# A fused attention and feed-forward kernel: the first two batches' w_in product by seven multiplications, part of it made ahead and kept in DRAM, and the opening loads re-dealt

## The chip, the cores and the metric

The kernel runs on one core of one Trainium2 chip. The metric is the device time of one execution in microseconds (us). Engines are TensorE (PE in the profile; PEld is its weight loading), VectorE (DVE), ScalarE (ACT), GpSimd (POOL) and SyncE (SP), which only issues transfers here.

## The reference, cut to what matters

```python
# q, k, v: (8 batches, 12 heads, 448, 64); w_in (768, 2048) and w_out (2048, 768) come as 64-bit floats
q_n, k_n = rmsnorm(q, g_q), rmsnorm(k, g_k)
attn = softmax(q_n @ k_n.T / 8) @ v
x = attn_out.transpose(0, 2, 1, 3).reshape(8 * 448, 768)
h = x @ w_in
out = (h * sigmoid(h)) @ w_out
```

The kernel walks over 48 *pairs* of heads (six per batch, n = 0 to 47). In each pair TensorE makes scores, weighted sums and transposes, ScalarE the exponentials, VectorE the sums of exponentials and GpSimd the power of the norms. Between them TensorE gets *filler*: x @ w_in of the two batches finished before. Two batches together need 16 x 12 multiplications of a 128 x 128 piece of w_in with x; "seven products" is the scheme that makes a 2 x 2 block product from seven multiplications rather than eight, at the price of additions, some of them of w_in itself (`sum_w_in`), some of x (`sum_x`).

## The kernel before: the parts concerned

w_in comes as 64-bit words and is rounded to 32 bits on the chip in 24 pieces. One rounding is two ScalarE copies ("opening"), three VectorE instructions and one GpSimd addition.

```python
    def round(self):                                             # class Rounder (cut)
        ...
            nc.vector.tensor_scalar(out=dst, in0=dst, scalar1=HIGH_MIN, scalar2=HIGH_MAX, op0=ALU.max, op1=ALU.min)      # L106
            nc.vector.tensor_scalar(out=wi, in0=wi, scalar1=3, scalar2=0x3FFFFFF8, ...)                                 # L109
            nc.vector.scalar_tensor_tensor(out=wi, in0=high, scalar=-(1 << 30), in1=wi, ...)                            # L113
            nc.gpsimd.tensor_tensor(out=wi, in0=wi, in1=low, op=ALU.add)                                                # L117
        while self.load():       # issues the next raw pieces on SyncE's queue (L68)
            pass
```

Row sums of the exponentials, their reciprocal and the division:

```python
    def sums(members, width):
        ...                                          # TensorE: ones x sums of exponentials (L444)
        nc.vector.reciprocal(out=r[0], in_=t)        # L448

    def divide(n, t):
        engine = nc.gpsimd if n < z.NPAIR else nc.vector      # GpSimd in batch 0
        x = xT(*pairs[n])
        engine.tensor_tensor(out=x, in0=x, in1=t, op=ALU.mult)
```

One block by seven products, of which `two` and `five` are the parts; each product goes through one of two banks named mm, and a bank is free again only after the addition or copy that reads it:

```python
        def two(self):
            nc.scalar.copy(self.p1, (yield from self.product("1")))
            plus((yield from self.product("2")), self.p1, self.done[1, 1])     # plus: VectorE

        def five(self, late=0):
            ...
            plus((yield from self.product("6", steps)), p1, u2)
            nc.scalar.copy(p5, (yield from self.product("5", steps)))
            plus((yield from self.product("7", steps)), u2, u3)
            nc.gpsimd.tensor_tensor(out=u2, in0=u2, in1=p5, op=ALU.add)
            nc.gpsimd.tensor_tensor(out=done[2, 2], in0=u3, in1=p5, op=ALU.add)
            plus((yield from self.product("3", steps)), u2, done[1, 2])
            plus((yield from self.product("4", steps)), u3, done[2, 1])
```

For batches 0 and 1, half the blocks were made whole (six matmuls each), beside batches 1 and 2; the other half by seven products:

```python
    def first_two():
        yield from whole(1, early)          # blocks 0-7 of batch 1; those of batch 0 ran beside batch 1
        for c in range(HW):
            sum_x([0, 1], c)
        yield from halves_in([0, 1], late)

    def weights_in(n, point):               # what of w_in is prepared in pair n, at four points of it
        if n < NPAIR:
            count = point == 3
        else:
            count = n < 5 * NPAIR // 2 and point % 2
        for _ in range(count):
            room.w_in.round()
            room.w_in.open()
        ...                                 # sums of w_in in batches 2 and 3
```

Of the kernel before, what the change touches and what calls it, by code (L numbers as in the profile page):

```python
# [13 lines left out]
ALU = mybir.AluOpType  # L14
# [107 lines left out]
class Room:  # L122
# [6 lines left out]
    def __init__(self, nc, pool, w_in, z):  # L129
# [11 lines left out]
        for i in range(self.NC):  # L141
            for c in range(z.NW):
# [3 lines left out]
                low = 6 + number % 2 if late else 16 + number % 2  # L146
# [4 lines left out]
                        (before.get(raw), bits[:, ds(raw * n, n)]),  # L151
                        bits[:, ts(low, self.COLS)],
                    )
                )
                before[raw] = number
# [14 lines left out]
def kernel(  # L170
# [58 lines left out]
    for t, g in ((gq2, g_q), (gk2, g_k)):  # L229
        for half in range(2):  # L230
            nc.scalar.dma_start(t[ds(half * D, D), :], g.rearrange("(d one) -> d one", one=1))
    load(state, 1)
    for i, g in enumerate((g_q, g_k)):
        nc.sync.dma_start(g1[:, i, :], g.rearrange("(one d) -> one d", one=1))
    room = Room(nc, const, w_in, z)
    while room.w_in.load():
        pass
    ident = const.tile([P, P], F32, name="ident")
# [3 lines left out]
    minus_half = const.tile([P, 1], F32, name="minus_half")  # L242
    nc.gpsimd.memset(minus_half, -0.5)
# [14 lines left out]
    nc.vector.scalar_tensor_tensor(  # L258
        out=gains, in0=gq2, scalar=float(D) ** -0.5, in1=gk2, op0=ALU.mult, op1=ALU.mult
# [10 lines left out]
    def arm():  # L270

        own = [dict(st) for st in state]
        r = copy.copy(room)
        r.w_in = copy.copy(room.w_in)
        return dict(
            tc=tc, nc=nc, z=z, pairs=pairs, state=own, load=lambda *a: load(own, *a), room=r,
            ring=ring, w_out=w_out, normal=(normal, rms), ident=ident, ones=ones, minus_half=minus_half, gains=gains,
            out=out,
        )
# [45 lines left out]
def bounded(  # L325
# [110 lines left out]
    def is_single(n):  # L436
        b, hp = pairs[n]
        return hp >= z.NPAIR - 2 and (b == 0 or b % 2 == 1)
# [11 lines left out]
    def divide(n, t):  # L450
        engine = nc.gpsimd if n < z.NPAIR else nc.vector
        x = xT(*pairs[n])
        engine.tensor_tensor(out=x, in0=x, in1=t, op=ALU.mult)
# [108 lines left out]
    def whole(b, blocks):  # L562

        for f in blocks:
            h = bank(S)
            assert room.w_in.rounded >= (f // room.CHUNK + 1) * z.NW
            for c in range(z.NW):
                nc.tensor.matmul(  # L568
                    h, room.w1(c, f), xT(b, c), start=(c == 0), stop=(c == z.NW - 1)
                )  # L570
                yield S
            t = staged()[:, 0:S]
            nc.scalar.activation(t, h, AF.Silu)
            save(f, b * S, t)
# [25 lines left out]
    def part_in(group, m, rows):  # L600

        chunk = 2 * m // room.CHUNK
        assert all((chunk, step) in summed for step in range(4))
# [19 lines left out]
    def halves_in(group, blocks, beside=lambda m: iter(()), begun=()):  # L623

        owed = []
        for m in blocks:
            if m < len(begun):
                rows, part = begun[m]

                late = int(alone and m == 0)  # L630
                columns, skip = part.five(late), 5 * (HW - late) * late
            else:
                rows = [staged() for _ in range(2)]
                part = part_in(group, m, rows)
                columns, skip = chain(part.two(), part.five()), 0
# [3 lines left out]
            for n in columns:  # L639
                count += 1  # L640
                if count > 0 and (count - 1) % each == 0:
                    if count > each:
                        activate(owed)
                    next(aside, None)
# [3 lines left out]
            owed = [(2 * m + i, group[0], rows[i]) for i in range(2)]  # L648
# [116 lines left out]

    def start(group):


        begun = []
        for m in range(2):  # L770
            rows = [staged() for _ in range(2)]
            begun.append((rows, part_in(group, m, rows)))
        return begun


    early, late = range(z.NF // 2), range(HF // 2, HF)

    def first_two():
        yield from whole(1, early)
# [313 lines left out]
```

## Time and profile before

Median 1469.49 us of three executions (1467.93 to 1470.61). The profiled execution has a span of 1465.1 us. From the trace I cut the run at the first score matmul of each pair and counted TensorE's instructions at the costs that the prediction derives (0.376 us for one 448-column product instruction, two of them per f32 matmul); "idle" is the length of a stretch less that work.

| stretch (us) | length | TensorE work | idle |
|---|---|---|---|
| start to first scores | 15.4 | | |
| batch 0 (n = 0 to 5) | 58.4 | 43.0 | 15.5 |
| batch 1 (n = 6 to 11) | 90.7 | 78.3 | 12.4 |
| batch 2 (n = 12 to 17) | 101.2 | 95.6 | 5.6 |
| batch 3 (n = 18 to 23) | 103.7 | 97.1 | 6.5 |
| pair 0 / pair 4 / pair 6 | 9.5 / 12.9 / 18.7 | 5.3 / 8.3 / 10.5 | 4.3 / 4.6 / 8.2 |

A stretch with much idle time has a hole that something other than TensorE makes. The lines of the profile behind this are in the prediction. The list of instructions in time order gives start, length, engine, line, operation, tiles, count. In the list of instructions in time order (start, length, engine, line, operation, tiles, count), the kernel before has its second group of eight score matmuls at

```profile
20.54 1.76 PE L400 MATMUL sc<-work 64*112 64x448 f32 x8
```

1.76 us is the length at full clock; the first eight, at 15.37, took 3.33 us at half clock.

### The profile page before, as it was taken

The page shows a single profiled execution, that of the slowest core. Times are in us where ns is not written, and L with a number is a line of the kernel's source. Part 1 is how long each engine was busy: PE and PEld are TensorE (multiplying, and loading weights), DVE is VectorE, ACT ScalarE, POOL GpSimd, SP SyncE. Part 2 cuts the span into 40 slices and gives each one's busy share as a digit, 9 for nine tenths or more (in the row PEclk, how much of TensorE's full clock was granted, in tenths as well). Part 3 has the DMA queues.
Part 4 walks back from the last instruction along what each step waited for, and adds up shares of the span by engine and source line. Part 5 has one row for each costly group of instructions (what it writes and reads, how often), then busy time and mean ns, then how long its engine had stood idle before and what let it go on. Part 6 is the DMA issues. An engine that isn't in the chain of part 4 may idle for free.

```text
span 1465.1 us, 14059 instructions
## 1 busy us (share of the span) xinstructions
PE 1432.2 (98%) x5048; PEld 698.8 (48%) x5048; DVE 693.9 (47%) x915; ACT 568.7 (39%) x931; POOL 395.5 (27%) x250
## 2 busy tenths in 40 slices
PE   5989999999999999999999999999999999999998
PEld 2334444444444444444444445555555555555554
DVE  4777866656644545744544687722222222222220
ACT  6779886455555455455445344300000000000000
POOL 5765451333233333332332044410000000000000
PEclk9999999999999999999999999999999999999999
DMA  7524432222232223222221157422222222222220
GB/s 220 131 83 136 140 103 75 78 73 66 71 96 73 67 72 98 63 72 87 76 60 67 63 169 240 138 94 79 79 79 79 81 81 84 81 81 86 85 65 25
DMA packets 124660, 135.49 MB, mean 92 GB/s; under 512 B 50660, under 2 KB 106788, under 8 KB 124580
## 3 DMA queue, kind: packets, MB, share of 16 engines
q1 hardware_dynamic: 124260, 134.49, 30.2%
q8 instruction: 42, 0.69, 0.2%
q14 instruction: 38, 0.31, 0.1%
q10 hardware_dynamic: 320, 0.00, 0.0%
HBM read 87.56 MB, written 40.37 MB: 87 GB/s over the span
## 4 chain that ended last, share of the span: by engine, by line
PE 91%; DVE 4%; issue 1%; POOL 1%; ACT 1%; DMA 0%; ACTq 0%; DVEq 0%; POOLq 0%
PE mm L527 36%; PE sc L527 14%; PE sc L400 9%; PE av L416 9%; PE av L527 7%; PE tr L527 7%; PE mm L568 4%; PE tr L386 2%; PE tr L444 1%; PE tr L381 1%; DVE work L428 1%; DVE work L448 1%; DVE rms L298 1%; POOL rms L304 0%; DVE sums_x L475 0%
## 5 line engine op out<-in xcount | busy, mean ns | idle before, releaser
L405 ACT ACTIVATE work<-sc,rms 112x448 f32<-112x448 f32 x384 | 212.3, 636 | 177.7 <-PE sc L400 154.7
L304 POOL TENSOR_TENSOR rms<-rms,minus_half 112x16 f32<-112x16 f32 (+1 forms) x49 | 175.9, 3590 | 292.3 <-DVE rms L300 271.4
L527 PE MATMUL mm<-x,W 128*128 128x448 f32 x552 | 220.8, 541 | 0.7 <-ACT stage L534 0.6
L400 PE MATMUL sc<-work 64*112 64x448 f32 x768 | 173.2, 570 | 1.4 <-ACT work L390 0.7
L527 PE MATMUL mm<-sums_x,W 128*128 128x448 f32 x408 | 165.9, 542 | 0.7 <-DVE stage L478 0.5
L416 PE MATMUL av<-work,rows 112*64 112x448 f32 x768 | 165.7, 552 | 0.0
L428 DVE TENSOR_TENSOR work<-work 112x896 f32<-112x896 f32 x144 | 158.8, 1104 | 1.8
L527 PEld LDWEIGHTS mm<-x,W 128*128 128x128 f32 x552 | 101.8, 190 | 93.1 <-issue 88.0
L547 POOL TENSOR_TENSOR parts<-parts,stage 128x448 f32<-128x448 f32 (+1 forms) x33 | 37.2, 1128 | 314.2 <-DVE parts L478 302.7
L400 PEld LDWEIGHTS sc<-work 64*112 64x112 f32 x768 | 61.8, 175 | 104.5 <-issue 79.4
L527 PEld LDWEIGHTS mm<-sums_x,W 128*128 128x128 f32 x408 | 74.8, 190 | 68.9 <-issue 61.5
L448 DVE RECIPROCAL work<-tr 128x448 f32<-128x448 f32 x25 | 73.9, 2956 | 49.6 <-PE tr L444 49.6
L416 PEld LDWEIGHTS av<-work,rows 112*64 112x64 f32 x768 | 46.6, 136 | 105.9 <-issue 99.5
L547 POOL TENSOR_TENSOR parts<-parts,W 128x384 f32<-128x384 f32 x9 | 9.0, 995 | 307.8 <-DVE parts L478 307.8
L568 PE MATMUL mm<-x,W 128*128 128x448 f32 x192 | 75.9, 541 | 0.0
L534 ACT COPY stage<-mm 128x448 f32<-128x448 f32 (+1 forms) x30 | 15.7, 524 | 150.0 <-PE mm L527 144.0
L478 DVE TENSOR_TENSOR stage<-mm,parts 128x448 f32<-128x448 f32 (+1 forms) x51 | 31.4, 615 | 78.5 <-PE mm L527 51.6
L527 PE MATMUL mm<-W,work 128*128 128x384 f32 x204 | 68.6, 486 | 0.0
L392 DVE TENSOR_SCALAR work<-tr,gains 128x448 f32<-128x448 f32 x36 | 24.6, 684 | 89.3 <-PE tr L386 89.3
L653 ACT ACTIVATE stage<-stage 128x896 f32<-128x896 f32 x56 | 51.2, 945 | 36.8 <-DVE stage L478 35.9
L527 PE MATMUL sc<-W,work 128*128 128x384 f32 x192 | 64.5, 486 | 0.0
L298 DVE TENSOR_REDUCE rms<-qn 112x8 f32<-112x512 f32 x49 | 33.3, 681 | 55.7 <-ACT qn L297 53.5
(159 smaller groups left out, 1898.8 us busy)
## 6 DMA issues: line engine op xcount, KB each, us to landing
hidden<-stage SPq DMA_DIRECT2D x56, 448.0 KB, 2.8
work<-hidden SPq DMA_DIRECT2D x7, 2048.0 KB, 9.0
x<-hidden SPq DMA_DIRECT2D x7, 2048.0 KB, 8.9
W<-in_moe_w_in_dram SPq DMA_DIRECT2D x24, 512.0 KB, 4.1
rows<-in_moe_w_out_dram SPq DMA_DIRECT2D x32, 384.0 KB, 3.4
rows<-in_q_dram SPq DMA_DIRECT2D x48, 224.0 KB, 3.1
rows<-in_k_dram SPq DMA_DIRECT2D x48, 224.0 KB, 3.6
rows<-in_v_dram SPq DMA_DIRECT2D x48, 224.0 KB, 2.7
```

The source lines that it names most:

```text
L298: nc.vector.tensor_reduce(out=rms[:, i], in_=t, axis=AX.X, op=ALU.add)
L304: nc.gpsimd.tensor_tensor(out=flat, in0=flat, in1=half, op=ALU.pow)
L400: nc.tensor.matmul(banks[:, h, 0:S], kT[rows, ts(j, R)], qT[n % 2][rows, :], start=True, stop=True,)
L405: nc.scalar.activation(e[j][:, h, :], banks[:, h, 0:S], AF.Exp, scale=rms[n % 4][:, 1, h, j : j + 1])
L416: nc.tensor.matmul(st["av"][ds(h * D, D), :], st["v"][:, h, j, :], e[j][:, h, :], start=(j == 0), stop=(j == J - 1),)
L428: nc.vector.tensor_tensor(out=t, in0=e[0] if j == 1 else t, in1=e[j], op=ALU.add)
L448: nc.vector.reciprocal(out=r[0], in_=t)
L478: nc.vector.tensor_tensor(out=out, in0=a, in1=b, op=ALU.add)
L527: nc.tensor.matmul(t, self.left(name, s), self.right(name, s), start=s == ends[0], stop=s == ends[1])
L547: nc.gpsimd.tensor_tensor(out=u2, in0=u2, in1=p5, op=ALU.add)
L568: nc.tensor.matmul(h, room.w1(c, f), xT(b, c), start=(c == 0), stop=(c == z.NW - 1))
L653: nc.scalar.activation(t, t, AF.Silu)
```

## The change

Its intent: make the first two batches wholly by seven products (fewer matmuls), of which only products 1 and 2 of two double blocks are made early, beside batch 1, and parked in a DRAM buffer; prepare w_in in other places to match (the last twelve roundings in pairs 13 to 16 in threes, sums of w_in in pairs 12, 13, 17 and 18); divide on VectorE in batch 0 too; drop batch 0's single row sums; and re-deal the small loads of the opening. The diff, cut to its core:

```diff
-    for t, g in ((gq2, g_q), (gk2, g_k)):
-        for half in range(2):
-            nc.scalar.dma_start(t[ds(half * D, D), :], ...)
+    for i, g in enumerate((g_q, g_k)):
+        nc.scalar.dma_start(g1[:, i, :], ...)                # for the branch
     load(state, 1)
-    for i, g in enumerate((g_q, g_k)):
-        nc.sync.dma_start(g1[:, i, :], ...)
...
+    for t, g in ((gq2, g_q), (gk2, g_k)):
+        for half in range(2):
+            nc.gpsimd.dma_start(t[ds(half * D, D), :], ...)  # the gains, now from GpSimd
...
-    nc.vector.scalar_tensor_tensor(out=gains, in0=gq2, scalar=float(D) ** -0.5, in1=gk2, ...)
+    nc.gpsimd.tensor_tensor(out=gains, in0=gq2, in1=gk2, op=ALU.mult)
+    nc.gpsimd.tensor_scalar(out=gains, in0=gains, scalar1=float(D) ** -0.5, ...)
...
     def is_single(n):
-        return hp >= z.NPAIR - 2 and (b == 0 or b % 2 == 1)
+        return hp >= z.NPAIR - 2 and b % 2 == 1
...
     def divide(n, t):
-        engine = nc.gpsimd if n < z.NPAIR else nc.vector
-        engine.tensor_tensor(out=x, in0=x, in1=t, op=ALU.mult)
+        nc.vector.tensor_tensor(out=x, in0=x, in1=t, op=ALU.mult)
...
-    def whole(b, blocks):                                    # removed
+    ahead = dram.tile([AHEAD, P, 2 * S], F32, name="ahead")
+    def make_ahead(group):
+        for m in range(AHEAD):
+            row = staged()
+            yield from part_in(group, m, [row, row]).two()
+            nc.sync.dma_start(ahead[m], row)
...
     def weights_in(n, point):
-        if n < NPAIR:
+        if n < 2 * NPAIR:
             count = point == 3
         else:
-            count = n < 5 * NPAIR // 2 and point % 2
+            count = 2 * NPAIR < n < 2 * NPAIR + 5 and point > 0
...
+        i = n - 2 * NPAIR
+        if i == 0 and point > 1:
+            for step in range(2):
+                sum_w_in(1, 2 * (point - 2) + step)
+        if i in (1, 5, 6):
+            sum_w_in({1: 0, 5: 2, 6: 3}[i], point)
```

Lines of the changed kernel are numbered four or five higher: the products L527 are L531, the additions that empty the banks L482, the division L457, the row sums L449.

## The prediction

> **What bounds the kernel now.** I read the page first, then stretches of time by batch, then the list of instructions in time order at the two ends of batch 0 and at the start of batch 4. On the page:
>
> ```profile
> PE 1432.2 (98%) x5048; PEld 698.8 (48%) x5048; DVE 693.9 (47%) x915; ACT 568.7 (39%) x931; POOL 395.5 (27%) x250
> PEclk9999999999999999999999999999999999999999
> L568 PE MATMUL mm<-x,W 128*128 128x448 f32 x192 | 75.9, 541 | 0.0
> L527 PE MATMUL mm<-x,W 128*128 128x448 f32 x552 | 220.8, 541 | 0.7 <-ACT stage L534 0.6
> ```
>
> TensorE is the bound, but its busy time is padded: these are spans of pipelined matmuls, so 98% is not full speed. What a matmul costs must come from a dense run:
>
> ```profile
> 373.20 4.69 PE L527 MATMUL mm<-x,W 128*128 128x448 f32 x12
> ```
>
> Twelve instructions in 4.69 us, of which the last shows its full 0.54: (4.69 - 0.54)/11 = 0.377 us each. L568 has 192 rows for what the source makes 96 matmuls (16 blocks x 6 steps), so an f32 matmul is two instructions: 0.752 us per matmul. I count TensorE work with this. Scores and weighted sums run two heads side by side (8 instructions in about 1.5 us plus the tail), so a pair of heads needs 32 x 0.188 + 8 transposes x 0.096 = 6.8 us, and 1.5 more in every second pair for the row sums.
>
> Then by batch, the borders being the first score matmul of batches 0 to 5:
>
> ```profile
> core 0: us, PE busy (x) PEld busy (x) DVE busy (x) ACT busy (x) POOL busy (x), PEclk, DMA share, GB/s
> 15.40:73.80 58.40, 53.27 (x252) 19.24 (x253) 40.11 (x53) 47.18 (x90) 44.49 (x23) 0.97 0.53 149
> 73.80:164.50 90.70, 85.57 (x354) 34.75 (x352) 69.61 (x87) 76.19 (x123) 48.74 (x27) 0.96 0.38 113
> 164.50:265.80 101.30, 100.85 (x399) 42.95 (x398) 68.09 (x93) 75.67 (x115) 38.42 (x19) 1.00 0.33 96
> 265.80:369.40 103.60, 102.23 (x405) 42.87 (x404) 66.07 (x77) 55.94 (x90) 38.54 (x20) 1.00 0.25 73
> ```
>
> Counting the instructions of each stretch at the costs above gives TensorE work of 43.0, 78.3, 95.6 and 97.1 us: idle time inside the stretches is 15.5, 12.4, 5.6 and 6.5 us. From batch 2 on each pair loses only about 1 us, so there a matmul added or removed shows in full. Batches 0 and 1 have real holes. The biggest is in the first pair of batch 1 (18.7 us for 10.5 of work), the next in pair 4 of batch 0 (12.95 for 8.3):
>
> ```profile
> 71.65 2.23 POOL L453 TENSOR_TENSOR x<-x,work 128x448 f32<-128x448 f32 x2
> 72.82 2.96 DVE L448 RECIPROCAL work<-mm 128x448 f32<-128x448 f32 x1 [3.87 <-POOL x L453]
> 75.92 2.12 POOL L453 TENSOR_TENSOR x<-x,work 128x448 f32<-128x448 f32 x1 [2.04 <-ACT work L297]
> 77.09 1.24 DVE L109 TENSOR_SCALAR W<-W 128x512 int32<-128x512 int32 x1
> 82.63 1.76 PE L444 MATMUL mm<-work,ones 112*64 112x448 f32 x4 [4.88 <-DVE work L428]
> ```
>
> GpSimd divides x by the row sums only after its slow power (3.7 us) and the q scaling; VectorE's next reciprocal waits for that (it overwrites the divisor), then all of VectorE is late, and TensorE's row sums wait 4.9 us. The clock is granted at 0.82 in this pair. The opening:
>
> ```profile
> 6.59 0.16 DVE L258 SCALAR_TENSOR_TENSOR gains<-gq,gk 128x1 f32<-128x1 f32 x1 [6.59 <-DMA gk<-in_g_k_dram]
> 8.18 3.26 POOL L304 TENSOR_TENSOR rms<-rms,minus_half 112x8 f32<-112x8 f32 x2 [6.79 <-DVE rms L300]
> 10.95 0.14 DVE L254 TENSOR_SCALAR small<-most 1x1 int32<-1x1 f32 x1
> 15.37 3.33 PE L400 MATMUL sc<-work 64*112 64x448 f32 x8 [0.62 <-ACT work L382]
> ```
>
> VectorE first waits for the gains, though the squares were done before; the branch, which every engine takes, waits for a comparison at the end of that queue.
>
> **What the Trainium skill says.** "TensorE: Matmul & The Clock Gate", section "HAM oscillation — how this bites in real kernels", has the matmul clock halved after idle gaps over about 3.4 us; the 0.82 of the stretch with the 4.9 us wait agrees. "SBUF — State Buffer", "Who interferes with whom": a GpSimd instruction and certain VectorE ones exclude each other for their whole length; agrees, the L109 above took 1.24 us beside a GpSimd division against 0.43 alone. "ScalarE: Activation LUTs", "What ACT_TABLE_LOAD costs": 1283 ns a load; the trace's loads between Silu and Exp take 1.28 us. "DMA: Bandwidth & Descriptors", "Specifications": first byte about 1 us for a transfer issued from GpSimd, about 0.6 from the other queues; no run here shows the former yet.
>
> **The change, part by part.**
>
> 1. Fewer products. Before: the first 8 blocks of w_in whole for batches 0 and 1 (96 matmuls), the rest by seven products (4 double blocks x 7 x 3 = 84), 180 in all. After: 8 x 21 = 168. Saved: 12 x 0.752 = 9.0 us of TensorE time, in stretches where it is the bound.
>
> 2. Where the products stand. Beside batch 1 there were 44 matmuls; now products 1 and 2 of two double blocks, 12. TensorE work of batch 1 falls from 78.3 by 24.1 to 54.2. Batches 2 and 3 go from 68 each to 78 each (156 = 168 - 12): +10 x 0.752 = 7.5 us each. The sum is again -9 us. What is not arithmetic is whether batch 1 really runs at its TensorE work. ScalarE per pair, by start-to-start times: 8 exps 4.3, two squares 1.06, three copies 1.6, opening one piece of w_in 1.13, a sixth of two copies 0.2: 8.3 us. The Silu instructions and 13 table loads (16.7 us) that batch 1 now has go. VectorE: adds 3.2, rounding 1.5, reductions 1.3, reciprocal 1.5, divisions 0.6, the rest 0.3: 8.4. TensorE: 8.3 and 9.8 in turn. Three engines close together, so I take the pace of batch 0's undisturbed pairs (8.85, 10.06, 7.77, 9.27 us at 7.2 of TensorE work) and about 1 us over TensorE: six pairs at 9.3 and 10.3 in turn, 59, and 1.5 for its start: 60.5. That is 30.2 off batch 1, 6 more than the removed work: the hole of its first pair closes, since the divisions move to VectorE and the single row sums of batch 0 (one reciprocal, 2.96 us) go.
>
> 3. Batch 0: pair 4 loses its wait behind GpSimd and the slow-clock scores (2.77 us for eight instead of 1.76), about 2.3 us; pair 5 loses a single row sum and its wait, 1.1. Together -3.4 us.
>
> 4. Batch 2 pays for the concentration. Its first pair is built like that of batch 4, which takes 17.7 us with VectorE busy all of it; now it has a rounding (1.55) and four sums of w_in (4 x 0.95) on top. Following VectorE's new order by hand, it enters the next pair some 4 us late; that pair has three roundings (4.7) and four sums (3.8) more. TensorE's seventh matmul of the filler then waits about 1.2 us for a bank, and by the pair after VectorE again waits for TensorE. I allow 1.5 us: batch 2 +7.2 (its own count is 77.5 against 68) +1.5 = +8.7; batch 3 +7.9 and nothing else: 78.5 against 68.
>
> 5. The rows kept in DRAM: two stores and two loads of 448 KB; stores of this size land in 2.8 us, and the load is issued about 12 matmuls, some 15 us, before its use. Hidden. The same for the ring of w_in pieces.
>
> 6. Opening. VectorE no longer waits for the gains, and the comparison comes early, so transposing k no longer waits for the normalised q. GpSimd now issues four small transfers and multiplies the gains before its powers. I take the powers from 8.2 to about 7, and from there: both powers 3.3, kT copy 0.7, q transposes 1.0, copy 0.6, gaps: scores at 12.9 to 13.2. -2.3 us.
>
> Sum: -2.3 - 3.4 - 30.2 + 8.7 + 7.9 = -19.3; I round to -18.5 for what I overlooked: 1469.5 - 18.5 = 1451 us.
>
> **Rivals.** (a) Batch 1 becomes bound by ScalarE, VectorE and the power on GpSimd, with TensorE too empty to hide their chains: pairs of 11 us instead of 9.9, 6.5 us worse, 1457. For it: batch 0 has 2 us idle per pair on that very loop. Against: part of that was the divisions on GpSimd. (b) VectorE's crowding in pairs 12 to 14 does not dissolve, each pair costing 2 to 3 us: 1456. For it: VectorE is full in the first pair of batch 4 already. Against: that pair costs TensorE only 1.15 idle. (c) The loads issued from GpSimd come late, with ident and ones behind them, so the opening gains nothing or loses 1 to 2 us: 1454. For: the skill's longer latency, four in a row; against: ScalarE issued its four in 2.5 us. (d) All goes well, both batches near their TensorE work and the opening at 12 us: 1444.
>
> **Range and chances.** The fixed part is the 9 us; the other 9 to 10 depend on holes closing in batches 0 and 1. Two of the rivals together give 1459, the lucky case 1443: that is the range. Faster by over 2% means under 1440.1, beyond the lucky case: 5%. Slower has no path but a stall of 48 us that nothing suggests: 1%. Within 2%: 94%.
>
> **What would show it.** In the changed kernel: 336 filler rows for the first two batches in place of 360; batch 1 60 us long with no Silu in it; batches 2 and 3 near 110 and 111.5; the pair of 18.7 us gone; first scores near 13 us; from batch 4 on nothing changed but the offset. Batch 1 over 66, or TensorE waiting for w_in's sums in batch 2, would prove me wrong in part 2 or 4; first scores later than 15.4, in part 6.

## The result, and the profile after

The changed kernel took 1463.43 us, median of four executions (1463.24 to 1464.18), against 1469.79 (1467.93 to 1470.61) for the kernel before. Ratios here are those for the fast runs of both kernels in the same rounds, so not quite the ratio of the medians: 0.9959, with a 95% interval of 0.9942 to 0.9977. The time lies above the predicted range of 1443 to 1459.

The page of the changed kernel, first the engines' busy times and instructions, then the largest group of products (busy time, mean ns of one, idle time before them and what ended most of it):

```profile
PE 1425.0 (98%) x5024; PEld 693.9 (47%) x5024; DVE 708.7 (48%) x939; ACT 540.5 (37%) x907; POOL 402.6 (28%) x258
L531 PE MATMUL mm<-x,W 128*128 128x448 f32 x648 | 261.1, 542 | 3.5 <-DVE parts L482 3.2
```

24 TensorE instructions fewer, 12 matmuls, as meant. What is new is the releaser: the group's waits are now put down to VectorE's additions L482, where before there was almost nothing. The table of stretches, borders again at the first score matmul of each batch:

```profile
core 0: us, PE busy (x) PEld busy (x) DVE busy (x) ACT busy (x) POOL busy (x), PEclk, DMA share, GB/s
14.60:71.60 57.00, 53.08 (x248) 19.56 (x248) 42.67 (x59) 47.07 (x90) 39.99 (x19) 1.00 0.58 160
71.60:136.10 64.50, 61.31 (x296) 22.50 (x294) 53.59 (x66) 49.64 (x95) 38.41 (x19) 1.00 0.40 114
136.10:255.40 119.30, 110.68 (x418) 46.19 (x418) 98.08 (x133) 69.53 (x115) 57.92 (x33) 1.00 0.39 115
255.40:365.70 110.30, 109.72 (x427) 46.70 (x426) 63.54 (x76) 59.53 (x96) 37.75 (x20) 1.00 0.27 81
```

| stretch (us) | before | after | TensorE work after | idle after | change measured | change predicted |
|---|---|---|---|---|---|---|
| to first scores | 15.4 | 14.6 | | | -0.8 | -2.3 |
| batch 0 | 58.4 | 57.0 | 42.2 | 14.8 | -1.4 | -3.4 |
| batch 1 | 90.7 | 64.5 | 55.0 | 9.5 | -26.3 | -30.2 |
| batch 2 | 101.2 | 119.3 | 103.1 | 16.2 | +18.0 | +8.7 |
| batch 3 | 103.7 | 110.3 | 104.6 | 5.7 | +6.7 | +7.9 |
| sum | | | | | -3.8 | -19.3 |

From batch 4 on nothing changed. The sum is 2.5 us less of a gain than the medians show, because the profiled execution of the kernel before was a quick one: 1467.17 us where its median is 1469.49.

In batch 2 VectorE is busy 98 of 119 us, against 68 of 101 before, and TensorE's idle time rises from 5.6 to 16.2 us. Lines chosen from pairs 14 to 16, in time order, show how:

```profile
193.91 1.24 DVE L106 TENSOR_SCALAR W<-W 128x512 f32<-128x512 f32 x1
194.83 1.32 POOL L551 TENSOR_TENSOR parts<-parts,stage 128x448 f32<-128x448 f32 x1
195.19 1.25 DVE L109 TENSOR_SCALAR W<-W 128x512 int32<-128x512 int32 x1
...
204.15 8.01 SPq L68 DMA_DIRECT2D W<-in_moe_w_in_dram  x2
210.13 0.42 DVE L106 TENSOR_SCALAR W<-W 128x512 f32<-128x512 f32 x1
210.24 1.79 ACT L662 ACTIVATE stage<-stage 128x896 f32<-128x896 f32 x2
210.59 0.43 DVE L109 TENSOR_SCALAR W<-W 128x512 int32<-128x512 int32 x1
211.05 0.69 DVE L113 SCALAR_TENSOR_TENSOR W<-W 128x512 int32<-128x512 int32 x1
211.66 0.62 DVE L482 TENSOR_TENSOR parts<-mm,stage 128x448 f32<-128x448 f32 x1
212.22 0.90 SPq L564 DMA_DIRECT2D hidden<-stage  x2
212.33 2.52 PE L531 MATMUL mm<-x,W 128*128 128x448 f32 x6 [1.57 <-DVE parts L482]
216.88 0.53 ACT L549 COPY stage<-mm 128x448 f32<-128x448 f32 x1 [4.85 <-DMA hidden<-stage]
```

Two things are to be read here. First, L482, the addition that empties a product's bank, stands in VectorE's queue behind the three instructions of a rounding; it ends at 212.28, and the products wait 1.57 us for it. Second, ScalarE needs the room of finished rows that are being stored; it waits 4.85 us and does not empty its bank until 216.88. SyncE issues in order, and these stores (L564) stand behind the second of two raw pieces of w_in, whose place is free only when the rounding has read it (L113 ends at 211.74). The line of 204.15 merges the two issues; the second waits from 204.61 and goes at 211.82, the stores at 212.22. That queue explains little of the 4.85 us, though: the rows themselves, the two Silu of L662, are ready only at 211.19 and 212.03, so the first store is 1.0 us late. By the trace it lands at 216.78, 4.6 us after its issue, with a raw piece issued just ahead of it. The other such wait, in pair 17, has no raw piece in front:

```profile
230.24 2.48 SPq L473 DMA_DIRECT2D work<-work  x4
231.49 1.79 ACT L662 ACTIVATE stage<-stage 128x896 f32<-128x896 f32 x2
233.85 1.19 SPq L475 DMA_DIRECT2D work<-work  x2
235.14 1.00 SPq L564 DMA_DIRECT2D hidden<-stage  x2
237.90 0.53 ACT L549 COPY stage<-mm 128x448 f32<-128x448 f32 x1 [4.62 <-DMA hidden<-stage]
```

There the first row is ready at 232.44 and its store goes 2.7 us later, behind six small copies of row sums (L473, L475).

The first three lines of the longer list show a further loss: beside a GpSimd addition the same two VectorE instructions take 1.24 and 1.25 us instead of 0.42 and 0.43. The list of waits of batch 2 (engine, tile and line, what it waited for: us in all, times, longest) sums it up; the last line is from the same list of SyncE's queue:

```profile
ACT stage L549 <- DMA hidden<-stage: 9.5, 2, 4.8
PE mm L531 <- DVE parts L482: 4.8, 5, 1.6
...
SPq L68 <- DVE W L113: 33.3, 7, 7.8
```

The opening of the changed kernel in time order:

```profile
6.31 0.98 PE L391 MATMUL tr<-ident,rows 112*128 112x112 f32 x4 [6.31 <-DMA rows<-in_k_dram]
8.54 0.19 POOL L262 TENSOR_TENSOR gains<-gq,gk 128x1 f32<-128x1 f32 x1 [4.31 <-DMA gk<-in_g_k_dram]
8.68 3.27 POOL L309 TENSOR_TENSOR rms<-rms,minus_half 112x8 f32<-112x8 f32 x2
12.27 0.64 ACT L395 ACTIVATE work<-tr,gains 128x448 f32<-128x448 f32 x1 [5.44 <-POOL gains L263]
14.59 3.33 PE L405 MATMUL sc<-work 64*112 64x448 f32 x8 [0.62 <-ACT work L387]
20.20 3.33 PE L405 MATMUL sc<-work 64*112 64x448 f32 x8
```

The branch is early as meant: k is transposed at 6.31, not 11.98. But GpSimd takes its queue in order, and the multiplication of the gains stands ahead of the powers: it waits for a small load until 8.54. The powers start at 8.68, later than the 8.18 of before. The 0.8 us won at 14.59 is then lost: the second eight scores, at 20.20, still run at half clock.

### The profile page after: what moved, and what is told of

It reads as the page before. It is cut to its first block, busy times and chain, and to the rows that moved or that the text cites. A ratio compares the mean times of both kernels' runs of the same rounds, so it can differ in the third digit from the quotient of the medians.

```text
span 1461.4 us, 13997 instructions
## 1 busy us (share of the span) xinstructions
PE 1425.0 (98%) x5024; PEld 693.9 (47%) x5024; DVE 708.7 (48%) x939; ACT 540.5 (37%) x907; POOL 402.6 (28%) x258
## 4 chain that ended last, share of the span: by engine, by line
PE 85%; DVE 4%; issue 1%; DMA 1%; ACT 0%; POOL 0%; SPq 0%; DVEq 0%; ACTq 0%; POOLq 0%
PE mm L531 38%; PE sc L531 14%; PE sc L405 8%; PE av L421 8%; PE av L531 7%; PE tr L531 7%; PE tr L449 1%; PE tr L391 1%; PE tr L386 1%; DVE work L433 1%; DVE rms L303 1%; DMA rows<-in_v_dram 0%; DVE work L453 0%; DVE stage L482 0%; DVE W L482 0%
## 5 line engine op out<-in xcount | busy, mean ns | idle before, releaser
L531 PE MATMUL mm<-x,W 128*128 128x448 f32 x648 | 261.1, 542 | 3.5 <-DVE parts L482 3.2
L531 PE MATMUL mm<-sums_x,W 128*128 128x448 f32 x480 | 195.2, 542 | 3.2 <-DVE parts L482 1.6
L531 PEld LDWEIGHTS mm<-x,W 128*128 128x128 f32 x648 | 118.5, 190 | 110.2 <-issue 98.9
L551 POOL TENSOR_TENSOR parts<-parts,stage 128x448 f32<-128x448 f32 (+1 forms) x37 | 41.8, 1129 | 327.5 <-DVE parts L482 323.1
L531 PEld LDWEIGHTS mm<-sums_x,W 128*128 128x128 f32 x480 | 87.7, 190 | 83.3 <-issue 70.6
L405 PEld LDWEIGHTS sc<-work 64*112 64x112 f32 x768 | 61.7, 174 | 103.7 <-issue 77.5
L482 DVE TENSOR_TENSOR stage<-mm,parts 128x448 f32<-128x448 f32 (+1 forms) x59 | 36.2, 616 | 83.5 <-PE mm L531 51.9
L662 ACT ACTIVATE stage<-stage 128x896 f32<-128x896 f32 x64 | 58.5, 945 | 36.6 <-DVE stage L482 35.7
L531 PE MATMUL mm<-W,work 128*128 128x384 f32 x204 | 68.6, 486 | 0.0
L531 PE MATMUL sc<-W,work 128*128 128x384 f32 x192 | 64.5, 486 | 0.0
L313 POOL TENSOR_TENSOR qn<-rows,rms 112x512 f32<-112x512 f32 x47 | 56.6, 1205 | 3.7
```

The source lines that it names most:

```text
L313: engine.tensor_tensor(out=by_head, in0=rows["q"], in1=factor, op=ALU.mult)
L405: nc.tensor.matmul(banks[:, h, 0:S], kT[rows, ts(j, R)], qT[n % 2][rows, :], start=True, stop=True,)
L482: nc.vector.tensor_tensor(out=out, in0=a, in1=b, op=ALU.add)
L531: nc.tensor.matmul(t, self.left(name, s), self.right(name, s), start=s == ends[0], stop=s == ends[1])
L662: nc.scalar.activation(t, t, AF.Silu)
```

## The experiments

Fourteen kernels were run. The stretches are counted as above. Those with "one execution" give one time and a profile; the others have four executions beside the kernel before. The rounds ran on different chips, and the kernel before had medians of 1469.06 to 1470.9 us in them (1469.79 beside the changed kernel), so totals of different rounds compare to some 2 us only. Stretches are each read from one profile.

### 1. Batch 2: is it the roundings? (`no_late_round`)

The last twelve pieces of w_in skip VectorE's and GpSimd's part of the rounding; loads, openings and filler stay. The result is wrong.

```diff
-        if src.dtype == I64:
+        if src.dtype == I64 and i < getattr(self, "plain_from", 99):
...
         self.w_in = Rounder(nc, pieces)
+        self.w_in.plain_from = 12
```

> Wrong result on purpose: the changed kernel without the rounding of the last 12 pieces of w_in (three VectorE instructions and one GpSimd add each; the ScalarE opening and the loads stay). In the changed kernel batch 2 took 119.3 us, 16.2 of them idle on TensorE, where 110 were predicted. Theory A (VectorE and GpSimd are overfull in the first five pairs of batch 2, and output banks come free late behind the roundings): batch 2 falls to 109 to 112 us, TensorE idle in it to 6 to 9, the run by 7 to 10 us to about 1454 to 1456. Rival B (the raw loads and the stores of hidden rows block each other in the one DMA queue, and ScalarE waits for a stage buffer): the loads still wait for ScalarE's opening only, so part of it goes too, but the waits of ScalarE on stores stay and batch 2 stays above 114. Rival C (the new block order and the fetched rows cost it): nothing changes, batch 2 at 118 to 120.

One execution: 1458.3 us. Batch 2 shrinks from 119.3 to 113.7 us, idle from 16.2 to 10.6; batches 1 and 3 stay at 64.4 and 110.3. The run was expected at 1454 to 1456 us and batch 2 at 109 to 112, so theory A was only about half of it. The stretch of batch 2 (columns as above: VectorE's busy time is the third, 74.7 us instead of 98.1):

```profile
136.90:250.60 113.70, 109.53 (x418) 46.48 (x418) 74.73 (x97) 69.52 (x115) 39.30 (x21) 1.00 0.41 121
```

So 5.6 of the 10.6 us of extra idle time come from these twelve roundings on VectorE and GpSimd. The rest is not theirs; one more rounding, the last of the first twelve, stays in pair 12.

### 2. Roundings and sums of w_in (`no_round_no_sums`)

In addition the sums of w_in are left out, and the products read raw quarters in their place. Wrong, with the same number of products.

```diff
+        self.w_in.plain_from = 12          # as in the kernel above
...
     def sum_w_in(i, step):
         summed.add((i, step))
+        return
...
-            "3": lambda c: s[:, 2, c],
+            "3": lambda c: room.w1(c, 2 * m),
             (5 and 6 likewise)
```

> Wrong result on purpose: the changed kernel without the rounding of the last 12 pieces and without the 16 sums of w_in (products 3, 5 and 6 take raw quarters instead); all matmuls and stores stay. Without the rounding alone batch 2 took 113.7 us with 10.6 idle on TensorE, 5.0 more idle than in the kernel before; pairs 12 and 13 still took 19.5 us each. Theory A (all of it is VectorE's queue): pair 12 falls to about 18, pair 13 to 18.3, batch 2 to 109.5 to 111. Rival (what is left is the block order and the stores, as 1.8 to 3 us of it went when the stores moved): batch 2 stays at 112.5 or more, pairs 15 and 17 at 18.9 and 19.

One execution: 1453.92 us, within 3 us of the prediction. Batch 2 is 111.6 us, idle 8.5, and VectorE is busy 64 us of it.

The load of these roundings and of the sums therefore accounts for 7.7 of the 10.6 us. Of the 2.8 that stay, some 1.8 are in pair 12 (2.9 us idle against 1.15 in the like first pair of batch 4; VectorE is busy 18.7 of its 19.5 us), and most of the rest is in pair 15, where ScalarE still waits 1.75 us for a store. Pair 12 did not fall to 18 as expected: its sums of w_in run only after pair 13 has begun, so taking them away leaves it as it was. VectorE's instructions in it are those of the first pair of batch 4 and one rounding more, 1.54 us, that neither experiment removed. That this rounding is the loss was not tested.

### 3. The same work, spread out (`spread_round`)

A correct kernel: the raw words of chunk 2 of w_in lie in the still empty place of chunk 3, and those of chunk 3 in the place of its own later sums, so that roundings need not come in threes: two per pair over pairs 13 to 19, sums of chunk 0 in pairs 13 and 14, of chunk 2 in pair 16, of chunk 3 in pair 20.

```diff
+    PLAN = {                                  # R round, O open, ij = step j of the sums of chunk i
+        0: ("", "", "10 11", "12 13"),
+        1: ("00", "R", "O 01", "R"),
+        2: ("O 02", "R", "O 03", "R"),
+        3: ("O", "R", "O", "R"),
+        4: ("O 20", "21", "R 22", "O 23"),
+        5: ("", "R", "O", "R"),
+        6: ("O", "R", "O", "R"),
+        7: ("", "O", "R", ""),
+        8: ("30 31", "32 33", "", ""),
+    }
```

> Right result: the changed kernel with the last 12 pieces of w_in rounded over seven pairs (two per pair instead of three in four pairs) and the sums of w_in spread; the raw words of the third quarter lie in the place of the fourth quarter, those of the fourth in the place of its own sums, so that the third quarter's sums need not wait for the fourth. VectorE work per pair in batch 2 is then by count 20, 14.4, 18.6, 16.3, 17.6, 12.6 us instead of 20.1, 17.8, 18.3, 17.9, 16.9, 13.3, some of it moved to batch 3. Theory A: batch 2 at 111 to 114 us and batch 3 at 110 to 112, the run 5 to 8 us shorter than the changed kernel (about 1456 to 1458). Rivals B and C: 2 us or less.

1462.83 us (1462.2 to 1463.74), ratio 0.9954 (0.9938 to 0.9971); batch 2 only falls to 117.5 us. Pairs 13 to 15 lose their holes (19.5, 18.5 and 18.9 us instead of 20.7, 19.2 and 21.1), but pair 17 grows to 21.6. There ScalarE waits 6.5 us for a store:

```profile
227.02 2.48 SPq L480 DMA_DIRECT2D work<-work  x4
228.48 1.79 ACT L669 ACTIVATE stage<-stage 128x896 f32<-128x896 f32 x2
232.16 0.85 SPq L571 DMA_DIRECT2D hidden<-stage  x2
236.80 0.53 ACT L556 COPY stage<-mm 128x448 f32<-128x448 f32 x1 [6.53 <-DMA hidden<-stage]
```

The first row is ready at 229.43; its store goes 2.7 us later, behind copies of row sums and one raw piece, and takes 4.5 us to land. SyncE's longest wait for a rounding, 11.0 us, begins only at 238.12 and ends before the next rows are ready (254.77), so it delays no store of finished rows. My expectation missed by leaving out SyncE's queue and the landing time.

### 4. The stores on another queue (`saves_on_act`, `spread_and_saves`)

Half the stores of finished rows (those of the first two batches) go out from ScalarE; first alone, then with the spread roundings.

```diff
     def save(f, column, t):
-        nc.sync.dma_start(hidden[f, :, ds(column, t.shape[1])], t)
+        queue = nc.scalar if column == 0 else nc.sync
+        queue.dma_start(hidden[f, :, ds(column, t.shape[1])], t)
```

> Right result: the changed kernel with the stores of the first two batches' hidden rows issued from ScalarE's queue (right behind the Silu that makes them) instead of SyncE's, where they stand behind raw loads that wait for roundings. In batch 2 of the changed kernel ScalarE waits 9.5 us for such stores. Removing the roundings took 5.6 of the 10.5 us of extra idle time away, so the crowding alone is not all of it. Theory B' (the blocked store queue is the second cause): batch 2 falls from 119.3 by 2 to 5 us to 114 to 117, mostly in pairs 15 and 17 (21.1 and 18.9 us), and the wait of ScalarE for stores falls under 4 us. Rival (VectorE alone: roundings and sums of w_in and x): batch 2 unchanged within 1 us.

One execution: 1464.05 us. ScalarE's wait for stores falls from 9.5 to 3.1 us and batch 2 by 1.9 to 117.4 (just short of the 2 to 5 expected), but batch 3 rises by 1.0. The stores now go out right behind the Silu, while SyncE still waits 37.1 us for roundings: what changed is what stands in front of the stores. The rest was eaten in batch 0, where the clock dropped once for 3.4 us (58.8 us instead of 57.0).

> Right result: both at once, the roundings spread over seven pairs and these stores on ScalarE's queue. In the spread version pair 17 took 21.6 us with 5.0 idle, and ScalarE waited up to 6.5 us for one store. Theory A with B': pair 17 at 17.5 to 19, batch 2 at 111 to 114 (117.5 when only spread), the run at about 1456 to 1459. Rival (VectorE alone): batch 2 stays at 116 to 118, the run at 1462.

1462.1 us (1461.28 to 1462.61), ratio 0.9938 (0.9921 to 0.9954). Batch 2 is 113.5 us, inside what was expected, and pair 17 is back to 17.6. Batch 3 takes 1.6 us of it back (111.9, since some roundings now lie there), and pair 0 and batch 0 were slow again (12.9 and 58.9 us), so the whole run missed the expected time. The two parts need each other: spreading alone takes 1.8 us off batch 2, moving the stores alone 1.9, both 5.8.

### 5. How much of the gain is the division? (`before_divide_vector`, `divide_back`)

In the kernel before, only the engine of the division is changed; in the changed kernel, only that is undone.

```diff
 before_divide_vector, against the kernel before
-        engine = nc.gpsimd if n < z.NPAIR else nc.vector
+        engine = nc.vector

 divide_back, against the changed kernel
-        nc.vector.tensor_tensor(out=x, in0=x, in1=t, op=ALU.mult)
+        engine = nc.gpsimd if n < z.NPAIR else nc.vector
+        engine.tensor_tensor(out=x, in0=x, in1=t, op=ALU.mult)
```

> The kernel before with the division of batch 0's x by the row sums moved from GpSimd to VectorE, nothing else. If the holes in pair 4 of batch 0 (12.95 us) and in the first pair of batch 1 (18.7 us) come from the divisions standing behind GpSimd's powers: pair 4 falls to about 10.6 and the first pair of batch 1 to 12 to 14, together 6 to 9 us off the run (1461 to 1464). If the single row sums (two reciprocals in a row) are the cause, the first pair of batch 1 stays above 16 and the run gains 3 us at most.

One execution: 1462.29 us, where the kernel before had 1469.06 in the same rounds. Pair 6 falls from 18.7 to 13.8 us, pair 4 from 12.9 to 11.1, batch 1 from 90.7 to 85.8. In this one execution the one line gives as much as the whole change.

> Right result: the changed kernel with the division of batch 0 back on GpSimd, all else as changed. The kernel before with this division alone moved to VectorE ran at 1462.3 us, as fast as the whole change (1463.4), so by that run the products, the DRAM rows and the opening earn nothing together. If the division carries the gain: the holes come back (pairs 4 to 6 of batch 0 and 1 from 30.1 us to 33 to 37) and the run is at 1466 to 1470. Rival (the shared row sums of the changed kernel had removed the cause already, so that both ways to close the hole are worth the same 5 to 7 us): pairs 4 to 6 lengthen by under 2 us and the run stays at 1463 to 1465.

1466.73 us (1465.66 to 1467.27), ratio 0.9977 (0.9961 to 0.9994). Pairs 4 and 6 go from 10.6 and 11.7 us to 12.9 and 12.8. Stretches of pair 4 in this kernel and in the changed one:

```profile
53.70:66.60 12.90, 11.14 (x51) 3.66 (x49) 8.87 (x10) 7.95 (x16) 9.05 (x6) 0.87 0.56 131
```

```profile
53.20:63.80 10.60, 9.61 (x50) 3.31 (x48) 9.14 (x9) 7.99 (x16) 6.87 (x4) 1.00 0.63 156
```

GpSimd is 2.2 us busier with the division, and the clock is granted at 0.87 instead of 1.00: the hole costs twice, once as a wait and once as slow matmuls after it. Undoing the division costs 3.3 us of the change's 6.4, so all the rest, nine microseconds of removed matmuls included, nets some 3 without it; but added to the kernel before, the division alone gives 6.8, and then the rest adds nothing (1462.29 against 1463.43). The shares do not add up because the division and the other edits close the same hole: pair 6 is idle 8.2 us before, 3.3 with the division moved alone, 3.0 with all but the division (single row sums gone, fewer products), 1.9 with everything. So the rival of the second expectation holds for pair 6, which lengthens by 1.1 us, and not for pair 4 (2.3).

### 6. The opening and pair 0 (`old_opening`, `fewer_first`)

`old_opening` is the changed kernel with the loads, the gains and the order of before. `fewer_first` keeps the new order but loads three pieces of w_in (512 KB each) before the loop and then two per rounding, to clear the way for the rows of the next pairs.

```diff
 old_opening
-    for i, g in enumerate((g_q, g_k)):
-        nc.scalar.dma_start(g1[:, i, :], ...)
+    for t, g in ((gq2, g_q), (gk2, g_k)):
+        for half in range(2):
+            nc.scalar.dma_start(t[ds(half * D, D), :], ...)
     ...                                    (gains on VectorE, g1 on SyncE, as before)

 fewer_first
-        while self.load():
-            pass
+        for _ in range(2):
+            self.load()
...
-    while room.w_in.load():
-        pass
+    for _ in range(3):
+        room.w_in.load()
```

> The changed kernel with the opening of the kernel before (gains' loads on ScalarE's queue, the two rows for the comparison on SyncE's, gains on VectorE). First scores back from 14.6 to 15.4 us. Theory D (the loads issued from GpSimd slow the first rows and all behind them, so pair 0 grew from 9.5 to 11.9 us and the new opening lost 1.6 us in all): pair 0 back to 9.5 us, and the run 1 to 2 us shorter than the changed kernel. Rival (pair 0 waits for rows that land late in any case, because 4 MB of w_in are ahead of them): pair 0 takes 11 us or more here too, or what starts later ends later, and the run is 0.8 us longer.

One execution: 1463.41 us, equal to the changed kernel. First scores at 15.8, pair 0 12.0 us, batch 0 56.4: pair 0 is as long with the old opening, and in the whole time the new opening neither gains nor loses. But the two are long for different causes. In `old_opening` the clock came to full speed at 26.7 us, the latest of all profiles, and ScalarE did not wait for the third pair's rows. It waits for them in none of the three profiles with the old opening, and 0.7 to 4.5 us in all ten with the new opening and eight pieces loaded first. So the new opening does make these rows late. Where full speed came early (18.2 to 18.7 us) pair 0 took 9.5 us with the old opening (the kernel before) and 11.8 and 12.8 with the new (`spread_kt`, `saves_on_act`), one profile each.

> Right result: the changed kernel with 3 instead of 8 pieces of w_in (512 KB each) loaded in the opening, and two per rounding after that. Pair 0 took 9.5 us in the one profile of the kernel before but 10.7 in another kernel with the same opening and 12.0 in the changed kernel with the old opening, so the opening's order isn't what lengthened it. Theory E (the rows of the third pair lie behind 4 MB of w_in in the transfers, and pair 0 waits for them): pair 0 falls from 12 to 8 to 9.5 us and the run by 2 to 3.5 us, to about 1460.5. Rival (pair 0 is bound by its own chain of powers and squares): pair 0 stays above 11, the run at 1463.

1463.63 us (1463.48 to 1464.22), ratio 0.9951 (0.9935 to 0.9968). Pair 0 is 11.2 us, not the 8 to 9.5 of the theory that w_in's loads hold it up; that theory falls.

The traces show two things that hold pair 0, of which either suffices. One is the clock: over all profiles it first reached full speed anywhere from 18.2 to 26.7 us after the start, and in `fewer_first` and the changed kernel (24.0 and 24.2) the second eight scores took 3.33 us. The other, with the new opening, is the rows of the third pair, which land behind the first 4 MB of w_in. In the profile of `spread_kt` (below) the clock happened to be full from 18.6; its list in time order:

```profile
19.92 1.76 PE L412 MATMUL sc<-work 64*112 64x448 f32 x8
22.17 0.63 ACT L309 ACTIVATE qn<-rows 112x512 f32<-112x512 f32 x1 [1.61 <-DMA rows<-in_q_dram]
26.50 1.76 PE L412 MATMUL sc<-work 64*112 64x448 f32 x8 [2.63 <-ACT work L402]
```

The scores are fast, but then ScalarE stands 1.61 us waiting for those rows, in front of the exponentials, and the next scores start at 26.50 us, when the changed kernel's do too. `fewer_first` lifted the rows without the clock. The kernel before had in its profile a full clock from 18.7 us and its rows in time. Experiment 9 lifts both.

### 7. Batch 1: do the row sums lack a bank? (`ones_bank`)

In batch 1 the row sums go into the banks of the products instead of the one bank of the transposes.

```diff
-        t = ps.tile([P, S], F32, name="tr") if members[0] >= z.NPAIR else bank(S)
+        t = ps.tile([P, S], F32, name="tr") if members[0] >= 2 * z.NPAIR else bank(S)
```

> Right result: the changed kernel with the row sums of batch 1 put into the product banks, as in batch 0, instead of the single transpose bank. Batch 1 took 64.4 us where 60.5 were predicted; in its even pairs (11.4 and 11.0 us) the row sums wait for ScalarE's copy of the transposed q out of that bank, a wait that four times as many products used to cover. If that wait is the 4 us: pairs 8 and 10 fall to 10.0 to 10.5, batch 1 to 62 or 63. Rival (the chain ScalarE squares, VectorE reductions, adds, row sums sets the pace, the bank is only the last link): pairs unchanged within 0.3 us, as the row sums then wait for VectorE's adds.

One execution: 1461.65 us; batch 1 is 64.4 us, unchanged to 0.1, so the bank is not what holds it. The 1.8 us against the changed kernel are no gain of batch 1: pair 12 is 1.3 shorter, pair 13 0.5 longer (VectorE is full in both), and batch 0 was 0.7 shorter.

### 8. Versions that should beat both (`spread_kt`, `spread_gpsimd_sums`)

`spread_kt` is `spread_and_saves` with the copy of the transposed k left on ScalarE for three pairs longer, which relieves VectorE in pair 12. `spread_gpsimd_sums` is that, with all sums of w_in but chunk 1's on GpSimd, and the gains multiplied after the powers.

```diff
 spread_kt
-            if n < 2 * z.NPAIR:
+            if n < 2 * z.NPAIR + 3:
                 nc.scalar.activation(kT, t, AF.Copy, scale=gains)

 spread_gpsimd_sums (further)
-            s[:, 0], s[:, 1], s[:, 2], (step,),
+            s[:, 0], s[:, 1], s[:, 2], (step,), nc.vector if i == 1 else nc.gpsimd,
...
+    normalise_rows(... the first pair ...)
     nc.gpsimd.tensor_tensor(out=gains, in0=gq2, in1=gk2, op=ALU.mult)      # moved behind it
```

> Right result: roundings spread, stores of the first two batches on ScalarE's queue (batch 2 at 113.5, batch 3 at 111.9), and besides the scaling of k's transpose left on ScalarE for three pairs longer (0.68 us of VectorE per pair in pairs 12 to 14, where VectorE was busy 20.1, 16.2 and 17.4 us and ScalarE 9.2, 9.4 and 15.2). Theory A: pairs 12 and 13 fall by 0.5 to 1 us each, batch 2 to 111.5 to 113, the run to about 1460 to 1461. If ScalarE's order delays k instead: no gain or up to 1 us worse.

1460.72 us (1460.27 to 1461.56), ratio 0.994 (0.9923 to 0.9957): 8.8 us below the kernel before in the same rounds (1469.56), as `spread_and_saves` was in its own (1470.9), so the total shows no gain of this edit. Pair 12 falls from 19.5 to 18.7, batch 2 to 112.7.

> Right result: as spread_kt, with the sums of three of the four quarters of w_in on GpSimd instead of VectorE (12 instructions of 0.95 us; about 1.9 on GpSimd by the 1.13 us of its 448-column adds), and the gains multiplied after the first powers instead of before. Theory A: batch 2 at 109.5 to 112 and batch 3 at 110.5; if GpSimd and VectorE exclude each other on such adds, VectorE loses as much as it is spared and batch 2 stays at 112 to 115. Opening: the powers start at about 5 to 7.7 us instead of 8.7 and the first scores at 12.5 to 13.5; the whole at 1457 to 1461.

1463.45 us (1461.88 to 1464.82), ratio 0.9953 (0.9937 to 0.997). The opening did what part 6 of the prediction had wanted: first scores at 12.5 us. But ScalarE then waited 4.5 us for the rows of the third pair, pair 0 took 15.2 us, and pair 2 began at 37.1, later than the 35.4 of the changed kernel. In batch 2, with the sums on GpSimd, pair 14 took 22.1 us, with a drop of the clock for 3.4 us. Together the moves lost 2.7 us by the medians; which lost how much is read from one profile, the slowest of the four executions.

### 9. Both holds of pair 0 lifted (`spread_kt_rows`, `spread_kt_rows_gains`)

What was still open is whether the late rows or the clock ate the early opening. `spread_kt` with the two edits of `fewer_first`; the second kernel also has the gains behind the powers, as shown above.

> The best version so far (1460.72 us) with only three pieces of w_in loaded first and two per rounding, so that the rows of the third pair aren't behind 4 MB of w_in. Theory F: pair 0 has two holds, the half clock of the second eight score matmuls and the late rows of the third pair, and lifting one alone shows little because the other ends at nearly the same time. Then the wait of ScalarE for these rows (0.5 to 2.6 us in the versions with all pieces first) is gone; if the clock reaches full speed before the second eight scores, pair 0 is 9 to 10 us and the run 1458 to 1459.5; if not, pair 0 is 11.2 to 11.5 and the run 1460 to 1461. Rival G: the rows don't matter at all; pair 0 stays at 11.5 to 13 whatever the clock does.

1460.38 us (1460.24 to 1462.26), ratio 0.9935 (0.9919 to 0.9952). In the profile the clock was full from 18.3 us, ScalarE's wait for rows was gone, and pair 0 took 9.6 us, as expected of two holds; pair 2 began at 32.9 us, where in `spread_kt` it began at 35.4. The run did not gain those 2.5 us. They were given back in pair 4, 13.5 us long instead of 10.4:

```profile
53.00 0.63 ACT L309 ACTIVATE qn<-rows 112x512 f32<-112x512 f32 x1 [1.19 <-DMA rows<-in_q_dram]
57.85 0.95 PE L456 MATMUL mm<-work,ones 112*32 112x448 f32 x6 [2.29 <-DVE work L440]
58.73 2.88 PE L412 MATMUL sc<-work 64*112 64x448 f32 x8
```

Again rows land late, now those of pair 6: the table of stretches gives the transfers a share of 0.93 to 1.16 between 49 and 55 us, with the pieces of w_in among them. ScalarE's squares come late, so VectorE's additions, so TensorE's row sums, which wait 2.29 us; and the clock drops for 3.4 us, so that eight scores take 2.88.

> The same, and the gains multiplied behind the powers, so that the first scores come at 12.5 us instead of 14.7 (as measured in spread_gpsimd_sums, where ScalarE then waited 4.5 us for the rows of the third pair and gave all of it back). Theory F: with the rows early the wait is gone, and most of the 2 us comes through: pair 2 starts at 31.5 to 33.5 us and the run takes 1457.5 to 1459.5. If the half clock alone sets the start (it ends at a time of its own, not after a number of matmuls), pair 0 takes 12 to 13 us, pair 2 starts at 34 to 35, and the run is 1460 to 1461. Rival G: pair 0 is again near 15 us, the run 1461 to 1463.

1461.19 us (1458.07 to 1462.91), ratio 0.9934 (0.9915 to 0.9954). First scores at 12.9 us, but the second eight at half clock (full from 24.1), pair 0 12.1 us, pair 2 at 32.8: the half clock took what the opening gave, and pair 4 was 13.5 us long again. Its four executions scatter by 4.8 us, and the mean granted clock goes with them: 0.999 at 1458.07 and 0.996 at 1462.91. Of the three versions none is told from the others by its interval; all beat the changed kernel's median by 2 to 3 us.

## Why the prediction was wrong, point by point

**The step that failed** is part 4: "by the pair after VectorE again waits for TensorE. I allow 1.5 us". VectorE was behind up to pair 17: extra idle time was 10.6 us, so batch 2 grew by 18.0 instead of 8.7. Rival (b) had the mechanism but sized it at 5 us. Skipping VectorE's and GpSimd's share of the roundings gives 5.6 us back, skipping the sums of w_in as well 2.1 more: shown. Through what: products wait for the addition that frees their bank, and that addition stands behind a rounding; this is read from the trace. And one thing no rival held: stores of finished rows go out late behind other issues of SyncE (1.0 us behind a raw piece that waits for a rounding, 2.7 us behind copies of row sums) and land up to 4.6 us later, and ScalarE waits for their room. Moving half the stores took 1.9 us off batch 2, and spreading alone fell short until that was done. The two figures overlap: without the roundings ScalarE's wait for stores falls too, from 9.5 to 5.0 us. The 2.8 us left are mostly in pairs 12 and 15; `spread_kt` took 0.7 off pair 12, and the split was not tested further.

**Part 1** was right: 24 instructions fewer, TensorE work of the four batches down by 9.1 us (9.0 predicted). **Part 5** was right of the rows kept in DRAM (no engine waits for them in the trace), but looked at these alone; the stores of finished rows were the trouble.

**Part 2** had the mechanism right and the size wrong by 3.9 us. The hole of pair 6 closed (18.7 to 11.7; the division or the other edits alone close most of it, as experiment 5 shows). But I put the even pairs at 10.3 us although my own count for them was 9.8 of TensorE work plus 1: pairs 8 and 10 took 11.4 and 11.0. The term that was mis-sized is "about 1 us over TensorE": the four pairs of batch 0 that it was taken from average 8.99 us, 1.8 over the 7.2 of work given for them, and batch 1 then measured 9.5 us idle, 1.6 per pair. And the last pair took 11.6, not 9.3: it has a row sum of its own that the two-step pattern left out, and TensorE waits for VectorE's additions there, in the list in time order:

```profile
127.98 2.21 DVE L433 TENSOR_TENSOR work<-work 112x896 f32<-112x896 f32 x2
130.34 0.97 PE L449 MATMUL tr<-work,ones 112*64 112x448 f32 x4 [1.18 <-DVE work L433]
```

That this chain, and not something else, sets the pace of batch 1 is argued from such lines; the one experiment on it only ruled out the bank.

**Part 3** was right for pairs 4 and 5 (-3.8 us against -3.4). Batch 0 as a whole missed by 2.0 because of pair 0, 2.4 us longer. No step of the prediction looked at pair 0. It is held by the half clock and by the third pair's rows, whichever ends later (experiments 6 and 9), and it is the new opening that makes those rows late; the profiled execution of the kernel before, with both early, was a quick one.

**Part 6** failed in one term: "I take the powers from 8.2 to about 7". They started at 8.68, because the multiplication of the gains stands ahead of them on GpSimd and waits for its load: rival (c). The larger error is that the term is worth nothing even when it comes true: with first scores at 12.5 and 12.9 us (experiments 8 and 9) the time did not fall. What starts earlier waits for rows, or runs at half clock, in pair 0 or in pair 4. That batch 0 as a whole is held by its transfers is argued from these waits; no run took w_in's loads out of it.

**The sum**: the misses of the stretches are +1.5, +2.0, +3.9, +9.3 and -1.2, together 15.5. The range allowed for two rivals of 3 to 6.5 us at once; (b) at twice its size, with (c) and half of (a), lay outside. Nine microseconds were really taken from the bound engine, and 14.8 (693.9 to 708.7 on the two pages) were handed to the engine that frees its banks, which in batch 2 alone got 30 us more.

## What to carry to other kernels

Work taken off the bound engine only counts if the engine that frees its buffers has room where the work now stands: follow that engine's queue pair by pair, over the whole stretch, before allowing a small stall. A queue that issues transfers in order is an engine too: what stands in front of a store holds it back, but compare with the time at which its data was ready before blaming the queue. Undo single lines of a change and apply them alone: here one line alone gave what the whole gave, and undone cost half of it, because the other edits closed part of the same hole.

## What the Trainium skill lacked or had wrong

- "TensorE: Matmul & The Clock Gate", "What's actually happening", has the clock change in windows of some 3.4 us and the change to full speed vary by 500 ns, and says that the number of slow matmuls differs between runs of one kernel. The window agrees: each drop of the clock inside the run lasted 3.4 or 6.8 us. But in this opening, with its gaps, full speed came anywhere from 18.2 to 26.7 us over the sixteen kernels profiled (first scores at 12.5 to 15.8), the same eight score matmuls took 1.76 or 3.33 us, and one kernel's executions ran from 1458.07 us at a mean granted clock of 0.999 to 1462.91 at 0.996.
- "SBUF — State Buffer", "Who interferes with whom": VectorE's rounding instructions took 1.24 and 1.25 us instead of 0.42 and 0.43 beside a GpSimd addition, as the page has it. Beside GpSimd's power (199.46 to 203.41 us, as far as spans on GpSimd can be trusted), two VectorE additions took 2.21 us and L106 took 0.41, the same as alone: a long GpSimd instruction on 16 elements does not hold VectorE off for its length.
- "DMA: Bandwidth & Descriptors", "Specifications", gives first bytes of about 1 and 0.6 us. What a kernel waits for was longer here: the small loads of the two gains landed 3.8 and 4.9 us after issue from GpSimd, 2.9 and 3.7 from ScalarE's queue (medians), with the opening's large loads beside them.
- I found on no page what GpSimd's power costs: 3.6 us for 112 x 16 elements.
